# Attention and mixture of experts on one core: how far ahead keys and queries are loaded, and queries in two transfers

## The chip, the cores and the metric

One NeuronCore of a Trainium2 chip runs the whole program. It has five engines that each work through their own list of instructions in order: TensorE (PE, with weight loads shown as PEld), VectorE (DVE), ScalarE (ACT), GpSimd (POOL) and SyncE (SP), which here does little but issue DMA transfers. The metric is the device time of one execution in microseconds, as the median of several runs.

## What is computed

Inputs are q, k and v of shape (4 batches, 8 heads, 768 positions, 64), one decay factor lam per head, and the weights of a mixture of 8 experts. The first part is attention with a decaying state, in blocks of positions; the second sends each of the 3072 rows to the one expert with the largest gate.

```
for each block of positions:                       # per batch and head
    intra = (q k^T * lam^(i-j), lower triangle) v
    inter = (q * lam^(i+1)) state
    out   = intra + inter
    state = lam^block * state + (k * lam^(block-1-j))^T v
x = out as 3072 rows of 512
e = argmax(x w_gate);  g = softmax(x w_gate)[e] * sigmoid(x w_output_gate)[e]
y = g * relu(x w1[e]) w2[e]                        # 512 -> 1024 -> 512
```

The kernel takes blocks of 128 positions, which gives the same result.

## The kernel before

The attention part is cut into 24 tiles: 6 blocks of 128 positions times 4 batches. Tile n is block n // 4 of batch n % 4 and holds all 8 heads. For each tile SP loads k (two transfers of 128 KB, heads 0 to 3 and 4 to 7, in runs of 256 bytes), q (one transfer of 256 KB) and v (one of 256 KB, in runs of 256 bytes). The rows of q lie as 8 consecutive positions of one head, 2 KB, in each of 128 partitions.

The loop runs over steps s = -2 to 21. Step s does the front half of tile s+2 (`stage_a`: PE transposes k and q, 4 transposes each, L323; ACT copies the key result, kT, L326, and the query result, qT, in four copies, L327, which also bring the positions back into their order), the score product of tile s+1 (`stage_b`, L360, with DVE's decay product into `at`, L369), and the rest of tile s (`stage_c1` and `stage_c`: the product with the state, L384, the product with v, L401, ACT's copy xT, L408, and the state's update). In step s DVE also turns the result of tile s-1 into rows, xn (`stage_d2`, L476), and SP stores them to a table x_d in DRAM (L478, called row store s-1 below). Every fourth step computes the gate's logits of four tiles, and DVE and POOL then work out where each row goes.

From step 17 on the expert part begins in between. SP reads the number of the first expert (TENSOR_LOAD of order_i) and loads its weights in pieces of 1 MB: raw_0 in step 17, raw_1 in step 18, raw_2 in step 20. In steps 20 and 21 POOL issues the first eight gathers (xg, L770), which fetch the first expert's rows from x_d; their row numbers are made by DVE in step 20, behind that step's other work. The first products of the experts wait for the eighth gather.

Three things set the order around the change. The first is the order in the code itself: the part runs under a manual schedule, so each engine's list is what the loop writes. The second is SP's list: k, q and v loads, row stores and weight pieces all stand in it one behind the other. Each transfer takes one of eight completion semaphores in turn (DMAHW0 to DMAHW7), and so waits for the transfer eight before it. The third is memory: tiles 0 to 15 load into eight buffers that later hold weights, tiles 16 and 17 into two of three raw buffers, tiles 18 to 21 into slots of 2 KB a partition. There are 44 slots, and kT, qT, kd, at, xT and xn take them in turn, so a copy into a slot may have to wait until the row store that last read it has landed.

What step s loads is told by two counters, one for k and q and one for v, which runs two tiles behind:

```
for i, m in ((0, n), (1, n - 2)):
    while loaded[i] <= min(m, NTILE - 1):
        load_qkv(loaded[i], *((0, 2), (2, 3))[i])
        loaded[i] += 1
```

Before the loop k and q of tiles 0 to 4 and v of tiles 0 to 2 are loaded (AHEAD is 5). In step s the call is `load_up_to(s + 5)`, one more from step 6 on and two more from step 11 on, so that step 6 loads tiles 11 and 12, and step 11 tiles 17 and 18.

Of the kernel before, what the change touches and what calls it, by code (L numbers as in the profile page):

```python
# [23 lines left out]
def kernel(  # L24
# [13 lines left out]
    nc = tc.nc  # L38
    B, H, S, D = q.shape
# [3 lines left out]
    NPAIR = H // 2  # L43
# [10 lines left out]
    AHEAD = 5  # L54
# [20 lines left out]
    def slot(name, dtype=F32):  # L75
        return pool.tile([P, 512], dtype, tag="slot", bufs=NSLOT, name=name)
# [68 lines left out]
    def load_qkv(n, i0=0, i1=3):  # L145
        if n >= NTILE:
            return
        c, b = divmod(n, B)
        ts = qkv.setdefault(n, [])
        if n not in packs:  # L150
            if n < EARLY + 2:
                tag, bufs = (("whi", 4), ("wlo", 4))[n % 2] if n < EARLY else ("raw", 3)
                t = wpool.tile([P, 4, 512], F32, tag=tag, bufs=bufs, name=f"qkv_{n}")
                packs[n] = [t[:, i, :] for i in range(4)]
            elif n >= NTILE - 2:
                ts2 = [pool.tile([P, 8 * P], F32, tag="wide", bufs=4, name=f"qkv_{n}_{i}") for i in range(2)]
                packs[n] = [t[:, 512 * i : 512 * i + 512] for t in ts2 for i in range(2)]
        for i, (nm, src) in list(enumerate((("k", k), ("q", q), ("v", v))))[i0:i1]:
            t = packs[n][i] if n in packs else slot(f"{nm}_{n}")
            rows = src[b, :, c * P : (c + 1) * P, :]  # L160
            if nm == "q":

                nc.sync.dma_start(t, rows.rearrange("h (s r) d -> h s (r d)", r=8))  # L163
            else:
                t = t.rearrange("p (h d) -> p h d", h=H)
                rows = rows.rearrange("h t d -> t h d")
                if nm == "k":
                    for y in range(2):
                        nc.sync.dma_start(t.rearrange("p (m y) d -> p y m d", y=2)[:, y], rows[:, 4 * y : 4 * y + 4])  # L169
                else:  # L170
                    nc.sync.dma_start(t, rows)
            ts.append(t)
# [46 lines left out]
    def decay_table():  # L219
        for h in range(H):  # L220
            nc.vector.tensor_tensor_scan(
                out=decay[:, h, :], data0=lamb[:, h : h + 1].broadcast_to([P, P]), data1=ident,
                initial=0.0, op0=ALU.mult, op1=ALU.add,
            )
        nc.vector.tensor_copy(
            out=kdec.rearrange("p (m y) o -> p y m o", y=2),
            in_=decay.rearrange("p (y m) t -> p y m t", y=2)[:, :, :, P - 1 : P],
        )
# [72 lines left out]
    def query_parts(pq):  # L301
        for j in range(2):
            for o in range(2):
                yield (
                    slice(j * D, (j + 1) * D),
                    lambda t, o=o: t.rearrange("p g (s m o) -> p g s m o", m=4, o=2)[:, :, :, :, o],
                    pq[o * D : (o + 1) * D].rearrange("p (m y g s) -> p y g s m", m=4, y=2, g=NPAIR)[:, j],
                )

    def stage_a(n):  # L310
# [37 lines left out]
    def stage_b(n):  # L348
        L = live[n]
        L["at"] = []  # L350
        if n < B:
            decay_keys(L["kd"], qkv[n][0])
        L["ps"] = [bank(f"ps_{n}_{j}") for j in range(2)]

        for m in range(4):
            for y in range(2):
                r = slice(y * D, (y + 1) * D)
                for z in range(2):
                    t = slice(z * D, (z + 1) * D)
                    nc.tensor.matmul(  # L360
                        L["ps"][y][t, m * P : (m + 1) * P], L["kT"][r, m, t], L["qT"][r, m, :], start=True, stop=True
                    )

    def stage_b2(n):
        L = live[n]
        dec = decay.rearrange("p (y m) t -> p y m t", y=2)
        for j, ps in enumerate(L.pop("ps")):
            at = slot(f"at_{n}_{j}").rearrange("p (g t) -> p g t", g=NPAIR)
            nc.vector.tensor_tensor(  # L369
                out=at, in0=ps.rearrange("p (g t) -> p g t", g=NPAIR), in1=dec[:, j], op=ALU.mult  # L370
            )
            weave()
            L["at"].append(at)
# [62 lines left out]
    def logits(n0, nb):  # L436
        parts = P // EG // nb
        pl = bank(f"pl_{n0}")
        for i in range(NPAIR // parts):
            for b in range(nb):  # L440
                xTv = xTs.pop((n0 + b)) if i == NPAIR // parts - 1 else xTs[n0 + b]
                xTv = xTv.rearrange("p (g t) -> p g t", g=NPAIR)
                for k in range(parts):
                    g = k * (NPAIR // parts) + i
                    r = (b * parts + k) * EG
                    nc.tensor.matmul(
                        pl[r : r + EG, 0:P], wgs[:, g, :], xTv[:, g], start=(i == 0), stop=(i == NPAIR // parts - 1)
                    )
        lT = small.tile([P, P], F32, tag="lT", name=f"lT_{n0}")
        nc.scalar.copy(out=lT, in_=pl[:, 0:P])  # L450
        lgs[n0] = (pl, lT, nb, parts)
# [149 lines left out]
    def at_once(steps):  # L601
        weave(len(later))
        for f in steps:
            f()
# [436 lines left out]
    with tc.manual_schedule():  # L1041
# [7 lines left out]
        def load_up_to(n):  # L1049
# [4 lines that stand above are left out]

        for s in range(-2, NTILE - 2):
            if s >= 0:
                load_up_to(s + AHEAD + (s >= 6) + (s >= 11))
            if s == -2:
                decay_table()
            if s == 0:  # L1060
                stage_b(1)
                stage_b2(1)
            rest = stage_a(s + 2)
            if late:
                late.pop(0)()
            if s >= 1 and s % B == 0:
                logits(s - B, B)
            for f in rest:
                f()
            if s >= 0:  # L1070
                stage_c1(s)
            if s == RES + 4:
                for j in range(4):
                    split_hi(0, j)
            stage_a2(s + 2)
            if s + 1 >= 0 and s != 0:
                stage_b(s + 1)
            n = s - 1
            if s >= 1 and s % B == 0:
                logit_rows(s - B)  # L1080
            if s + 1 >= 0 and s != 0:
                stage_b2(s + 1)
            if n >= 0 and n % B == B - 1:
                at_once(route_choose(n + 1 - B, n + 1))
                ranking = route_place(n + 1 - B, n + 1)
                per_turn[0] = 3 if n >= RES - 1 else 2
            if s == RES + 1:
                weave(len(later))
                expert_regs(0, order_i, 1)
                load_piece(0)  # L1090
            if s == RES + 2:
                load_rows(0, 0, 2, nc.gpsimd)
            if s == RES + 4:
                row_index(0)
                gather(0, 0, 3, RES * P)
            if s == RES + 5:
                gather(0, 3, 8, RES * P)
            if 0 <= n < LAST:
                stage_d2(n)
            if s == 0:  # L1100
                later.extend(inter_tables())
                routing_tables()
                order_tables()
            if s == 1:
                weave(len(later))
            if s == 2:
                blank_rows()
            if s >= 0:
                stage_c(s)
            if ranking and s != RES:  # L1110
                late.append(ranking[0])
                later.extend(ranking[1:])
                ranking = []
            if ranking:
                first_steps = pick_first() if s == RES else []
                for f in first_steps[:1] + ranking[:-2]:
                    f()
                place_scatter(len(pending))
                later.extend(first_steps[1:] + ranking[-2:])
                ranking = []  # L1120
            if s == RES + 2:
                load_piece(1)
            if s == RES + 4:
                load_piece(2)
            if s <= RES:
                place_scatter(1 if s < RES - 2 else 2)
# [99 lines left out]
        for p in range(E):  # L1226
# [3 lines left out]
            rows = p not in TURNED  # L1230
# [41 lines left out]
            for i, j in enumerate(steps):  # L1272
# [10 lines left out]
                m = max(ns - 1, 1)  # L1283
# [108 lines left out]
```

## Time and profile before

| | us |
|---|---|
| median of 3 runs | 438.67 (438.56 to 441.32) |
| the profiled execution | 439.27 |
| its span | 437.7 |
| PE busy | 403.2 (92%) |
| DVE, POOL, ACT busy | 284.9, 233.6, 188.7 |
| chain that ended last: PE, DMA, DVE, SP | 71%, 11%, 6%, 5% |
| DMA moved | 79.40 MB, 181 GB/s on average |

All numbers of the profile are from the one profiled execution, which took 0.6 us more than the median; between its span and its time lie 1.57 us. The attention part ends near 126 us, and the experts take the rest. In the views below a time is counted from the span's start; "L163" is line 163 of the kernel; the bracket at the end of a row gives how long the engine stood idle before it and what ended that. SPq rows are SP's issues of transfers; a long one is SP being held up before the transfer is taken. DMA share is the mean busy share of the 16 DMA engines; it can exceed 1 where packets overlap.

### The profile page before, as it was taken

The numbers are of one execution on the slowest core, as the hardware profiler recorded it, in microseconds if no ns is written. First come the engines' busy times: TensorE is split into PE (matmuls) and PEld (weight loads), VectorE is DVE, ScalarE is ACT, GpSimd is POOL, SyncE is SP. The second block draws the span as 40 slices with busy tenths as digits, with TensorE's granted clock in tenths as the row PEclk, the third lists the DMA queues.
The fourth block names the chain that finished last, engine by engine and source line by source line (L and its number), as shares of the span: only waits on it lengthen the run. The fifth ranks groups of instructions, "written<-read, shape, count | busy, mean of one in ns | idle before, by whom it ended". The sixth has DMA issues, their size and how long they took to land.

```text
span 437.7 us, 10404 instructions
## 1 busy us (share of the span) xinstructions
PE 403.2 (92%) x3816; PEld 367.1 (84%) x3816; DVE 284.9 (65%) x823; ACT 188.7 (43%) x455; POOL 233.6 (53%) x284
## 2 busy tenths in 40 slices
PE   5899999779946999989999999999999999999993
PEld 2778788668735979679999999999999989989983
DVE  2558587757567953486967976886785774774610
ACT  3675576446723512244604623532642552542400
POOL 4155868556574387768558366366366446311011
PEclk9999999989985999989999999999999999999998
DMA  7999899899952145564447945964964876361001
GB/s 141 186 213 256 224 227 240 193 248 234 332 189 78 49 108 197 166 220 157 127 134 224 299 144 173 291 221 146 297 218 130 258 252 219 127 207 55 1 26 49
DMA packets 91710, 79.40 MB, mean 181 GB/s; under 512 B 58877, under 2 KB 65025, under 8 KB 91649
## 3 DMA queue, kind: packets, MB, share of 16 engines
q1 hardware_dynamic: 84448, 62.39, 50.5%
q0 software_dynamic: 7056, 16.24, 12.0%
q8 instruction: 32, 0.52, 0.5%
q14 instruction: 30, 0.24, 0.2%
q10 hardware_dynamic: 144, 0.00, 0.0%
HBM read 62.45 MB, written 16.55 MB: 181 GB/s over the span
## 4 chain that ended last, share of the span: by engine, by line
PE 71%; DMA 11%; DVE 6%; SPq 5%; POOL 3%; issue 2%; ACT 1%; POOLq 0%; DVEq 0%; ACTq 0%
PE ph_None L80 9%; PE ph_None L81 9%; PE ph_None L79 9%; PE py L79 5%; PE py L80 5%; PE py L81 5%; DMA xg<-x_d,rows 4%; PE pyr L80 4%; PE pyr L81 4%; PE pyr L79 4%; DMA qkv<-in_q_dram 3%; PE ps L360 2%; PE po L401 2%; SPq L169 2%; SPq L163 2%
## 5 line engine op out<-in xcount | busy, mean ns | idle before, releaser
L770 POOL DMA_INDIRECT xg<-x_d,rows x103 | 114.6, 1112 | 72.6 <-issue 35.2
L133 DVE TENSOR_TENSOR wlo<-raw,whi 128x512 fp32r<-128x512 f32 x128 | 84.6, 685 | 0.7 <-ACT whi L124 0.6
L837 ACT ACTIVATE hhi<-ph_None 128x400 fp32r<-128x400 f32 (+4 forms) x56 | 28.0, 501 | 119.5 <-PE ph_None L81 114.6
L79 PE MATMUL ph_None<-xhi,whi 128*128 128x400 f32 (+4 forms) x224 | 76.9, 343 | 2.1 <-ACT xhi L801 2.1
L80 PE MATMUL ph_None<-xlo,whi 128*128 128x400 f32 (+4 forms) x224 | 76.9, 343 | 0.3 <-DVE xlo L805 0.3
L81 PE MATMUL ph_None<-xhi,wlo 128*128 128x400 f32 (+4 forms) x224 | 76.8, 343 | 0.0
L124 ACT CAST whi<-raw 128x512 fp32r<-128x512 f32 x128 | 74.4, 614 | 1.2 <-DMA raw<-in_moe_w_dram 1.2
L838 DVE SCALAR_TENSOR_TENSOR hlo<-ph_None,hhi 128x400 fp32r<-128x400 f32 (+4 forms) x56 | 31.8, 567 | 35.2 <-ACT hhi L837 34.9
L369 DVE TENSOR_TENSOR at<-ps,decay 128x512 f32<-128x512 f32 x48 | 31.4, 686 | 33.4 <-PE ps L360 33.1
L79 PEld LDWEIGHTS ph_None<-xhi,whi 128*128 128x128 f32 x224 | 42.6, 190 | 3.0 <-ACT xhi L801 2.6
L79 PE MATMUL py<-hhi,whi 128*128 128x400 f32 (+2 forms) x128 | 44.4, 347 | 0.0
L81 PE MATMUL py<-hhi,wlo 128*128 128x400 f32 (+2 forms) x128 | 44.4, 347 | 0.0
L80 PE MATMUL py<-hlo,whi 128*128 128x400 f32 (+2 forms) x128 | 44.4, 347 | 0.0
L80 PEld LDWEIGHTS ph_None<-xlo,whi 128*128 128x128 f32 x224 | 42.5, 190 | 1.0 <-DVE xlo L805 0.6
L327 ACT COPY qT<-pq 64x256 f32<-64x256 f32 x96 | 37.6, 392 | 12.1 <-PE pq L323 6.2
L81 PEld LDWEIGHTS ph_None<-xhi,wlo 128*128 128x128 f32 x224 | 42.5, 190 | 0.3
L954 POOL DMA_INDIRECT out_dram<-yn,table x12 | 12.7, 1056 | 49.9 <-DVE yn L1014 32.6
L80 PE MATMUL pyr<-wlo,hhi 128*128 128x512 f32 (+2 forms) x96 | 37.5, 390 | 0.0
L81 PE MATMUL pyr<-whi,hlo 128*128 128x512 f32 (+2 forms) x96 | 37.5, 390 | 0.0
L79 PE MATMUL pyr<-whi,hhi 128*128 128x512 f32 (+2 forms) x96 | 37.5, 390 | 0.0
L801 ACT CAST xhi<-y 128x256 fp32r<-128x256 f32 (+3 forms) x64 | 19.8, 362 | 39.6 <-DVE y L787 31.4
L613 POOL DMA_INDIRECT tab_d<-rec,idx x24 | 24.8, 1035 | 21.6 <-issue 14.2
(181 smaller groups left out, 761.8 us busy)
## 6 DMA issues: line engine op xcount, KB each, us to landing
raw<-in_moe_w_dram SPq DMA_DIRECT2D x29, 1024.0 KB
qkv<-in_k_dram SPq DMA_DIRECT2D x40, 128.0 KB
qkv<-in_q_dram SPq DMA_DIRECT2D x20, 256.0 KB
qkv<-in_v_dram SPq DMA_DIRECT2D x20, 256.0 KB
x_d<-xn SPq DMA_DIRECT2D x20, 256.0 KB
raw<-in_moe_w_dram POOLq DMA_DIRECT2D x3, 1024.0 KB
yd<-yo SPq DMA_DIRECT2D x12, 256.0 KB
yr<-yd SPq DMA_DIRECT2D x48, 64.0 KB
```

Of the source, the lines that this page charges most:

```text
L79: nc.tensor.matmul(ps, a[0], b[0], start=first, stop=False)
L80: nc.tensor.matmul(ps, a[0], b[1], start=False, stop=False)
L81: nc.tensor.matmul(ps, a[1], b[0], start=False, stop=last)
L124: nc.scalar.copy(out=hi, in_=src)
L133: eng.tensor_tensor(out=lo, in0=src, in1=hi.bitcast(F32), op=ALU.subtract)
L327: copies = [lambda r=r, view=view, src=src: nc.scalar.copy(out=view(qT[r]), in_=src) for r, view, src in query_parts(pq)]
L369: nc.vector.tensor_tensor(out=at, in0=ps.rearrange("p (g t) -> p g t", g=NPAIR), in1=dec[:, j], op=ALU.mult)
L613: nc.gpsimd.indirect_dma_start(out=tab_d, out_offset=bass.IndirectOffsetOnAxis(ap=idx, axis=0), in_=rec, in_offset=None, bounds_check=P * ...
L770: nc.gpsimd.indirect_dma_start(out=xg[(p, b // 4)][:, (b % 4) * P : (b % 4 + 1) * P], out_offset=None, in_=x_q[0 : 4 * rows], in_offset=ba ...
L801: nc.scalar.copy(out=hi, in_=src)
L837: nc.scalar.activation(out=hi[:, r], in_=ph[:, r], func=AF.Relu)
L838: nc.vector.scalar_tensor_tensor(out=lo[:, r], in0=ph[:, r], scalar=0.0, in1=hi[:, r].bitcast(F32), op0=ALU.max, op1=ALU.subtract,)
```

## The change

Two things change. First, `load_up_to` is called with s + 5 up to step 3 and with s + 4 from step 4 on, with nothing added later. Step 4 therefore loads nothing, and each later step loads one tile's k and q, four ahead of the step, and one tile's v, two ahead. Second, q comes in two transfers of 128 KB. Each covers four heads; a partition holds 4 consecutive positions of one head, 1 KB, per transfer. The transposes stay; the four copies of `query_parts` read the transposed result in another order, each from half of its columns.

```
-                nc.sync.dma_start(t, rows.rearrange("h (s r) d -> h s (r d)", r=8))
+                rows = rows.rearrange("(y m) (s r) d -> y s m (r d)", y=2, r=4)
+                for j in range(2):
+                    nc.sync.dma_start(t[:, 256 * j : 256 * j + 256], rows[j])
...
-                    lambda t, o=o: t.rearrange("p g (s m o) -> p g s m o", m=4, o=2)[:, :, :, :, o],
-                    pq[o * D : (o + 1) * D].rearrange("p (m y g s) -> p y g s m", m=4, y=2, g=NPAIR)[:, j],
+                    lambda t, o=o: t.rearrange("p g (s i o) -> p g s i o", i=2, o=2)[:, :, :, :, o],
+                    pq[o * D : (o + 1) * D, 256 * j : 256 * j + 256].rearrange("p (i s g) -> p g s i", i=2, g=NPAIR),
...
-                load_up_to(s + AHEAD + (s >= 6) + (s >= 11))
+                load_up_to(s + AHEAD - (s >= 4))
```

On SP, between row stores 9 and 10, before (qkv_17, k_18 and so on are the loads of those tiles; x_d<-xn_9 is row store 9; the brackets name the semaphores waited for):

```order
L478 DMA x_d_72<-xn_9_1273 128x512 [waits DMAHW7_49,DVE_49]
L169 DMA qkv_17_1303<-in_k_dram 128x4x64 [waits DMAHW0_49]
L169 DMA qkv_17_1303<-in_k_dram 128x4x64 [waits DMAHW1_49]
L163 DMA qkv_17_1303<-in_q_dram 128x1x512 [waits DMAHW2_49]
L169 DMA k_18_1307<-in_k_dram 128x4x64 [waits DMAHW3_49]
L169 DMA k_18_1307<-in_k_dram 128x4x64 [waits DMAHW4_49]
L163 DMA q_18_1310<-in_q_dram 128x1x512 [waits DMAHW5_49]
L171 DMA qkv_15_1108<-in_v_dram 128x8x64 [waits DMAHW6_49]
L171 DMA qkv_16_1215<-in_v_dram 128x8x64 [waits DMAHW7_49]
L478 DMA x_d_72<-xn_10_1366 128x512 [waits DMAHW0_49,DVE_49]
```

The same place on SP now:

```order
L480 DMA x_d_72<-xn_9_1278 128x512 [waits DMAHW6_49,DVE_49]
L171 DMA qkv_15_1308<-in_k_dram 128x4x64 [waits DMAHW7_49,PE_49,Pool_49]
L171 DMA qkv_15_1308<-in_k_dram 128x4x64 [waits DMAHW0_49]
L165 DMA qkv_15_1308<-in_q_dram 128x1x256 [waits DMAHW1_49]
L165 DMA qkv_15_1308<-in_q_dram 128x1x256 [waits DMAHW2_49]
L173 DMA qkv_13_1111<-in_v_dram 128x8x64 [waits DMAHW3_49]
L480 DMA x_d_72<-xn_10_1366 128x512 [waits DMAHW4_49,DVE_49]
```

The loads of tiles 16, 17 and 18, and v of tiles 14 to 16, now stand behind row store 10.

On SP, around the first weight pieces, before (row store 14 to raw_0; order_i holds the experts' numbers):

```order
L478 DMA x_d_72<-xn_14_1789 128x512 [waits DMAHW4_49,DVE_49]
L169 DMA qkv_23_0_1819<-in_k_dram 128x4x64 [waits DMAHW5_49]
L169 DMA qkv_23_0_1819<-in_k_dram 128x4x64 [waits DMAHW6_49]
L163 DMA qkv_23_0_1819<-in_q_dram 128x1x512 [waits DMAHW7_49]
L171 DMA v_21_1824<-in_v_dram 128x8x64 [waits DMAHW0_49,PE_49,Activation_49]
L478 DMA x_d_72<-xn_15_1923 128x512 [waits DMAHW1_49,DVE_49]
L171 DMA qkv_22_1_1731<-in_v_dram 128x8x64 [waits DMAHW2_49]
L663 TENSOR_LOAD order_i_145 [waits DVE_49]
L663 ISA x2
L111 ISA
L111 DMA raw_0_2059<-in_moe_w1_dram 128x4x512 [waits DMAHW3_49]
```

And now (raw_0 to the keys of tile 23):

```order
L111 DMA raw_0_2066<-in_moe_w1_dram 128x4x512 [waits DMAHW0_49]
L480 DMA x_d_72<-xn_16_2068 128x512 [waits DMAHW1_49,DVE_49]
L171 DMA qkv_22_0_2095<-in_k_dram 128x4x64 [waits DMAHW2_49]
L171 DMA qkv_22_0_2095<-in_k_dram 128x4x64 [waits DMAHW3_49]
L165 DMA qkv_22_0_2095<-in_q_dram 128x1x256 [waits DMAHW4_49]
L165 DMA qkv_22_0_2095<-in_q_dram 128x1x256 [waits DMAHW5_49]
L173 DMA v_20_2101<-in_v_dram 128x8x64 [waits DMAHW6_49]
L480 DMA x_d_72<-xn_17_2156 128x512 [waits DMAHW7_49,DVE_49]
L111 ISA
L111 DMA raw_1_2183<-in_moe_w1_dram 128x4x512 [waits DMAHW0_49,PE_49,Pool_49]
L171 DMA qkv_23_0_2185<-in_k_dram 128x4x64 [waits DMAHW1_49]
L171 DMA qkv_23_0_2185<-in_k_dram 128x4x64 [waits DMAHW2_49]
```

The loads of tile 22 stood two row stores ahead of raw_0 and now stand behind it; those of tile 23 stand behind raw_1. Row stores 14 to 16 now come before both.

On ACT, the copies of tiles 17 and 18, before (kT and qT are written to slots):

```order
L326 COPY kT_17_1747<-pk_17_1737 128x512 [waits PE_49,Activation_49]
L327 COPY qT_17_1748<-pq_17_1738 64x256 [waits DMAHW0_49,PE_49]
L327 COPY qT_17_1748<-pq_17_1738 64x256 x3
L408 COPY xT_15_1792<-po_15_0_1754 128x256 [waits PE_49,Pool_49]
L408 COPY xT_15_1792<-po_15_1_1755 128x256 [waits PE_49]
L326 COPY kT_18_1836<-pk_18_1826 128x512 [waits DMAHW5_49,DVE_49,PE_49]
```

And now:

```order
L328 COPY kT_17_1746<-pk_17_1736 128x512 [waits PE_49,Activation_49]
L329 COPY qT_17_1747<-pq_17_1737 64x256 [waits PE_49,Pool_49]
L329 COPY qT_17_1747<-pq_17_1737 64x256 x3
L410 COPY xT_15_1791<-po_15_0_1753 128x256 [waits PE_49]
L410 COPY xT_15_1791<-po_15_1_1754 128x256 [waits PE_49]
L328 COPY kT_18_1836<-pk_18_1826 128x512 [waits PE_49,Activation_49]
```

Before, qT of tile 17 waits on DMAHW0, the semaphore of row store 10, and kT of tile 18 on DMAHW5, that of row store 11; now neither waits for a transfer, as the slots come round in another order.

## The prediction

> **What bounds the kernel now.** I read the page first: how long, and where TensorE has holes.
>
> ```profile
> span 437.7 us, 10404 instructions
> PE   5899999779946999989999999999999999999993
> DMA  7999899899952145564447945964964876361001
> ```
>
> From slice 12 on (131 us) PE is nearly always full, and the change touches nothing there. Ahead of it stands the attention stage, with DMA near nine tenths, a dip of PE in slices 7 and 8, and a hole in slices 11 and 12. Next the table of stretches around both (us, then busy time of PE, PEld, DVE, ACT, POOL, then granted clock, DMA share, GB/s).
>
> ```profile
> 72.00:78.00 6.00, 6.00 (x137) 5.48 (x140) 5.80 (x23) 4.20 (x13) 3.89 (x6) 1.00 0.97 235
> 84.00:90.00 6.00, 4.83 (x105) 4.08 (x108) 1.30 (x5) 2.17 (x6) 3.49 (x4) 1.00 0.86 218
> 90.00:96.00 6.00, 3.53 (x57) 3.07 (x49) 3.58 (x7) 3.33 (x10) 3.09 (x3) 0.76 0.85 214
> 126.00:132.00 6.00, 0.00 (x0) 0.00 (x0) 1.80 (x3) 0.00 (x0) 4.85 (x7) 0.61 0.59 190
> ```
>
> Until 78 PE and DMA are both full. From 84 to 96 neither is. From 126 to 132 PE does nothing. PE's own order of time, with ACT's, shows the first dip (tiles 17 and 19 at their key transposes, then the query transposes of 19 to 23):
>
> ```profile
> 79.95 0.66 PE L323 MATMUL pk<-ident,qkv 128*128 128x128 f32 x4
> 83.94 1.09 PE L401 MATMUL po<-at,qkv 128*64 128x128 f32 x16 [1.43 <-DMA qkv<-in_v_dram]
> 96.53 0.64 PE L323 MATMUL pk<-ident,k 128*128 128x128 f32 x4
> 97.01 0.60 PE L323 MATMUL pq<-ident,q 128*128 128x128 f32 x4
> 100.99 0.60 PE L323 MATMUL pq<-ident,q 128*128 128x128 f32 x4
> 104.97 0.60 PE L323 MATMUL pq<-ident,q 128*128 128x128 f32 x4
> 109.66 0.60 PE L323 MATMUL pq<-ident,qkv 128*128 128x128 f32 x4
> 114.44 0.60 PE L323 MATMUL pq<-ident,qkv 128*128 128x128 f32 x4
> ...
> 86.08 1.55 ACT L327 COPY qT<-pq 64x256 f32<-64x256 f32 x4 [4.80 <-PE pk L323]
> 91.48 0.58 ACT L326 COPY kT<-pk 128x512 f32<-128x512 f32 x1 [3.18 <-DMA x_d<-xn]
> ```
>
> Two steps (15 and 16) take 96.53 - 79.95 = 16.6 us. Undisturbed ones take 3.98 (97.01, 100.99, 104.97), and one of the two has 1.0 us of logits: 9.0. So 7.6 us are lost. The 4.80 is put down to PE, which had finished its transposes long before; that copy (qT of tile 17) stands in the order behind the semaphore of x_d_10, the next (kT of tile 18) behind that of x_d_11. Both wait for a slot whose row store hasn't landed. Why it is late, SP's order of time says:
>
> ```profile
> 59.53 2.03 SPq L169 DMA_DIRECT2D qkv<-in_k_dram  x2
> 72.79 1.05 SPq L169 DMA_DIRECT2D qkv<-in_k_dram  x2
> 77.28 2.68 SPq L171 DMA_DIRECT2D qkv<-in_v_dram  x2
> 80.06 2.76 SPq L478 DMA_DIRECT2D x_d<-xn  x1
> 84.68 0.62 SPq L163 DMA_DIRECT2D q<-in_q_dram  x1
> 105.28 0.43 SPq L171 DMA_DIRECT2D qkv<-in_v_dram  x1
> 107.11 0.73 SPq L111 DMA_DIRECT2D raw<-in_moe_w_dram  x1
> ```
>
> SP opens step 8 at 59.53 and step 11 at 72.79: 4.42 us a step, for 1 MB. x_d_10, which belongs to step 11, goes out at 80.06, when PE is in step 15: SP runs four steps behind, since the transfers in front of it fill the DMA queue. At last the chain of waits (start, us, what):
>
> ```profile
> 85.89 5.49 DMA x_d<-xn
> 97.07 5.44 DMA qkv<-in_q_dram
> 126.55 6.41 DMA xg<-x_d,rows
> ```
>
> The q load of tile 22 lands at 102.51; the last of eight gathers, at 132.96, ends PE's hole.
>
> **The prices.** Two stretches of the DMA view, first one with large packets alone (115 to 118 us), then the mix (54 to 78):
>
> ```profile
> q1 hardware_dynamic: 605, 1.18, 102.5%
> ...
> DMA packets 13200, 5.65 MB, mean 235 GB/s; under 512 B 11898, under 2 KB 11898, under 8 KB 13195
> ...
> q1 hardware_dynamic: 13035, 5.56, 97.1%
> ```
>
> A 2 KB packet takes 1.025 x 16 x 3 us / 605 = 81 ns of one engine. In the mix, 13200 - 11898 = 1302 are large (106 us of 373), which leaves 22.8 ns for each 256 B packet. Over 16 engines: k or v of a tile (1024 packets) 1.46 us, q or a row store (128 packets) 0.65, a weight piece (512 packets) 2.60. A step is 1.46 + 1.46 + 0.65 + 0.65 = 4.22, against 4.42 measured. So the queue is a line in which each transfer has its price, and a transfer lands later or earlier by what is put ahead of it.
>
> **Part by part.** *Fewer loads ahead.* In front of x_d_10 three tiles' k, q and v drop out: 3 x (1.46 + 0.65 + 1.46) = 10.7 us. It then goes out as soon as DVE has it, and the 7.6 us go. What is late next is the loads themselves: each now has more row stores ahead of it. Tiles 9 to 17 have one or two, which may cost PE a us or two at single steps; from tile 18 on it is three, 3 x 0.65 = 1.95 us, and what PE lost earlier is inside that, since the line sets the pace.
>
> *The weight pieces.* raw_0 now stands ahead of tile 22's k and q (2.60 us), raw_0 and raw_1 ahead of tile 23's (5.20).
>
> *Queries in 1 KB rows.* The bytes are the same, and 256 packets take the place of 128. No row has a 1 KB packet. Through the two measured sizes goes the line 14.5 ns + 0.0325 ns a byte: 47.8 ns, twice that is 14.6 more than 81, or 0.12 us a tile. Ends: 0 if only bytes count, 0.65 if each packet costs as a 2 KB one. I take the line, since both its points are measured. Over tiles 5 to 22, 18 x 0.12 = 2.1 us. [...]
>
> *Start.* In the first microseconds the queue isn't full, and SP's issues set the pace.
>
> ```profile
> L169 SPq DMA_DIRECT2D qkv<-in_k_dram x40: 367/507/1817, 0.9 to 100.6; - x40
> L163 SPq DMA_DIRECT2D qkv<-in_q_dram x20: 621/1366/2656, 2.0 to 101.3; - x20
> L171 SPq DMA_DIRECT2D qkv<-in_v_dram x20: 422/455/2179, 4.5 to 109.3; - x20
> L327 ACT COPY qT<-pq x96: 377/392/411, 7.8 to 118.2; 64x256 f32<-64x256 f32 x96
> L408 ACT COPY xT<-po x48: 357/372/387, 16.7 to 124.8; 128x256 f32<-128x256 f32 x48
> ```
>
> Two more issues stand ahead of tile 2's loads, at 0.507 each: 0 to 1.0, and I take 0.6. Later they hide in SP's waiting for the queue.
>
> *Copies.* qT's copies read PSUM in another order. Today's strided ones take 392 ns, contiguous ones 372; the new order is worth 0 to 20 ns either way, and ACT is busy 4.20 of 6: 0. That the first two copies need half the transposes saves under 0.3 us, behind kT's copy: 0.
>
> *Sum.* The q of tile 22 lands at 102.51 + 1.95 + 2.60 + 2.1 + 0.6 = 109.8, less what the queue wins back from its dip between 84 and 96: 6 x (0.97 - 0.86) + 6 x (0.97 - 0.85) = 1.4. That is 108.4. Does it set the step? Tile 19's q went out by 85.30; at 5 us to landing (the two loads and stores in the chain took 5.44 and 5.49 from issue) it lands at 90.3, and now 1.95 + 15 x 0.12 + 0.6 - 0.7 = 3.7 later: 94.0. From there PE needs 109.66 - 97.01 = 12.65 and would be ready at 106.7. So tile 22 sets step 20, at 108.4 for 109.66: 1.3 us won of 7.6. Tile 23's follows a step's 4.42 and raw_1's 2.60 behind, at 115.4 for 114.44: 1 us late, and PE's idle 6 us (126 to 132) cover that. The gathers hang on step 20 through the expert's row numbers:
>
> ```profile
> 116.91 1.15 POOL L770 DMA_INDIRECT xg<-x_d,rows  x1 [2.75 <-issue]
> ```
>
> So 1.3 us pass on to the end. The profiled execution took 439.27, 0.6 above the median of 438.67: 439.27 - 1.3 - 0.6 = 437.4. Its own range, with 1 KB packets at 0, the dip not won back, and the start from 0 to 1: 434.9 to 439.9.
>
> **Rivals.** *Loads keep up (20%).* The 7.6 us all stay won: 431.1. It takes the q of tile 22 by 102, so a queue that carries 1 MB a step in about 4 us. For it speaks that the prices add up to 4.22 and not 4.42; against it the DMA share of 0.97 with three steps' time behind it. Half of it gives 434.9.
>
> *The weight pieces hold up the last tiles (15%, slower).* Between 105.28 + 0.43 and 107.11 SP reads the expert's number: 1.4 us in which nothing is issued, now ahead of tile 22. With that, no gain from the dip (1.4) and a 1 KB packet midway to its upper end (0.13 more a tile, 2.3), q lands at 108.4 + 5.1 = 113.5, 3.8 behind its need: 442.5. It decides from 109.66 on. Against it: eight transfers are under way while SP reads.
>
> *SP's issues are the bound (7%, slower).* SP's rows stand almost without gaps up to 107. If a half costs what the shortest q does (0.62), tiles 5 to 22 add 11 us, q of 22 lands at about 117 and the end is 446. Against it: v, with the same bytes in eight times the runs, takes a median of 0.455 where q takes 1.366, so the long issues are waiting. [...]
>
> *It changes nothing* (2%): the lag behind DVE stays. The forecast has 56%.
>
> **The numbers.** About 1% (4.4 us) is what can be told from no change. Faster by more, under 434.3: 0.17 of the first rival and 0.02 of the forecast, 0.19. Slower, over 443.1: the 0.07, and 0.05 of the weight pieces, 0.12. Within: 0.69. The range leaves out SP's 0.07 and some 0.11 of the first rival: 433.0 to 442.8.
>
> **What would show it.** Right: ACT's 4.80 and 3.18 gone; steps 15 and 16 in about 9 us; row store 10 issued near 70; PE waiting for q in steps 17 to 20 instead; q of tile 22 behind raw_0; the first gather near 115.6. A mean DMA packet price as before with 6144 more packets between 512 B and 2 KB shows the third term. Wrong: no wait for q after step 17 (the first rival), a first gather after 118 (the second), or SP steps over 4.9 us with a DMA share under 0.9 (the third).

## The result, and the profile after

The changed kernel takes 430.64 us (median of 428.38, 431.63, 429.66 and 432.49), the kernel before 438.62 in four runs: a ratio of 0.985 [0.981, 0.990]. Here and below a ratio, with its 95% interval in brackets, compares fast runs of both kernels alone, and so is not the quotient of the two medians. The forecast was 437.4 with a range of 433.0 to 442.8, so the time lies below the range. It lies at the first rival's figure (431.1), but it got there in another way, as shown below. The profiled execution took 428.38, 10.9 less than the one of before; the medians differ by 8.0.

The page of the changed kernel, in the slices of the span:

```profile
span 426.8 us, 10434 instructions
...
PE   8999999979769989799999999999999999999993
...
DMA  7899899989942172744368746946855975371001
```

PE starts with 8 and 9 where it had 5 and 8, and its deepest slice in the middle is a 6 where it was a 4. The stretches where the first dip and the hole lay (us, then busy time of PE, PEld, DVE, ACT, POOL, then granted clock, DMA share, GB/s):

```profile
84.00:90.00 6.00, 3.60 (x74) 3.30 (x74) 5.86 (x23) 2.34 (x8) 3.32 (x5) 0.93 0.86 240
90.00:96.00 6.00, 6.00 (x118) 5.26 (x112) 3.98 (x18) 3.17 (x9) 3.80 (x4) 0.79 0.88 202
126.00:132.00 6.00, 5.09 (x42) 4.47 (x42) 5.43 (x29) 1.92 (x6) 2.32 (x4) 0.66 0.47 171
```

From 84 to 90 a dip is left, even a little deeper than before (3.60 for 4.83). From 90 to 96 PE is full again, and from 126 to 132 the experts run already. Where the time was won shows in the query transposes. First of the kernel before (tiles 0, 1, 3, 5, 6, 7 and 17), then of the changed one (tiles 0, 1, 3, 6, 7, 17, 19, 22, and both transposes of 23):

```profile
7.08 0.66 PE L323 MATMUL pq<-ident,qkv 128*128 128x128 f32 x4 [1.22 <-DMA qkv<-in_q_dram]
10.34 0.66 PE L323 MATMUL pq<-ident,qkv 128*128 128x128 f32 x4 [1.22 <-DMA qkv<-in_q_dram]
18.30 0.63 PE L323 MATMUL pq<-ident,qkv 128*128 128x128 f32 x4 [1.18 <-DMA qkv<-in_q_dram]
26.23 0.63 PE L323 MATMUL pq<-ident,qkv 128*128 128x128 f32 x4 [0.44 <-DMA qkv<-in_q_dram]
30.40 0.63 PE L323 MATMUL pq<-ident,qkv 128*128 128x128 f32 x4 [0.43 <-DMA qkv<-in_q_dram]
35.68 0.60 PE L323 MATMUL pq<-ident,qkv 128*128 128x128 f32 x4
80.44 0.60 PE L323 MATMUL pq<-ident,qkv 128*128 128x128 f32 x4
```

```profile
5.82 1.06 PE L325 MATMUL pq<-ident,qkv 128*128 128x128 f32 x4
7.83 0.60 PE L325 MATMUL pq<-ident,qkv 128*128 128x128 f32 x4
15.17 0.70 PE L325 MATMUL pq<-ident,qkv 128*128 128x128 f32 x4 [0.31 <-DMA qkv<-in_q_dram]
26.29 0.60 PE L325 MATMUL pq<-ident,qkv 128*128 128x128 f32 x4
31.55 0.60 PE L325 MATMUL pq<-ident,qkv 128*128 128x128 f32 x4
76.27 0.60 PE L325 MATMUL pq<-ident,qkv 128*128 128x128 f32 x4
88.28 0.60 PE L325 MATMUL pq<-ident,q 128*128 128x128 f32 x4
102.09 0.60 PE L325 MATMUL pq<-ident,qkv 128*128 128x128 f32 x4
107.81 0.63 PE L325 MATMUL pk<-ident,qkv 128*128 128x128 f32 x4 [1.35 <-DMA qkv<-in_k_dram]
109.79 1.09 PE L325 MATMUL pq<-ident,qkv 128*128 128x128 f32 x4 [1.35 <-DMA qkv<-in_q_dram]
```

The first 4.1 us are won by tile 6 (30.40 to 26.29), whose loads go out in step 1, where both kernels load alike: PE waited for q at five of the first seven tiles, and hardly does now. From tile 7 to tile 17 nothing is won: 44.76 us before (80.44 - 35.68), 44.72 after. Tiles 17 to 19 then take 12.0 us (88.28 - 76.27) where they took 16.6 (97.01 - 80.44): 4.6 more. The last tiles give some of it back, so that tile 23 is 4.7 us ahead (114.44 and 109.79), but the first gather goes out before its queries are there. The first gather of the changed kernel, then the experts' first product before and after:

```profile
109.12 1.15 POOL L772 DMA_INDIRECT xg<-x_d,rows  x1 [2.52 <-PE pk L325]
```

```profile
134.19 0.58 PE L79 MATMUL ph<-xhi,whi 128*128 128x256 f32 x1 [9.17 <-ACT xhi L801]
```

```profile
124.22 0.58 PE L79 MATMUL ph<-xhi,whi 128*128 128x256 f32 x1 [3.86 <-ACT xhi L803]
```

The gather comes 7.8 us earlier (116.91 to 109.12), the product 10.0, the end 10.9.

The DMA view from 4 to 26 us, before and after:

```profile
DMA packets 11735, 4.07 MB, mean 185 GB/s; under 512 B 10984, under 2 KB 10984, under 8 KB 11733
...
q1 hardware_dynamic: 11733, 4.04, 94.5%
```

```profile
DMA packets 14517, 4.76 MB, mean 217 GB/s; under 512 B 12759, under 2 KB 14488, under 8 KB 14515
...
q1 hardware_dynamic: 14515, 4.73, 89.8%
```

17% more bytes a second, at a smaller share of the engines' time. That is not what a change of 128 into 256 packets should do, and it is what the experiments are about.

### The profile page after: what moved, and what is told of

It reads as the page before. It is cut to its first block, busy times and chain, and to the rows that moved or that the text cites. A ratio compares the mean times of both kernels' runs of the same rounds, so it can differ in the third digit from the quotient of the medians.

```text
span 426.8 us, 10434 instructions
## 1 busy us (share of the span) xinstructions
PE 402.1 (94%) x3816; PEld 366.9 (86%) x3816; DVE 285.0 (67%) x823; ACT 189.0 (44%) x455; POOL 233.6 (55%) x284
## 4 chain that ended last, share of the span: by engine, by line
PE 73%; DMA 11%; DVE 5%; SPq 4%; issue 2%; POOL 2%; ACT 0%; POOLq 0%; DVEq 0%
PE ph_None L80 9%; PE ph_None L81 9%; PE ph_None L79 9%; PE py L81 6%; PE py L79 6%; PE py L80 6%; DMA qkv<-in_q_dram 5%; PE ps L362 4%; PE pyr L80 3%; PE pyr L79 3%; PE pyr L81 3%; PE po L403 3%; PE po L386 2%; DMA xg<-x_d,rows 2%; SPq L171 2%
```

## Experiments

The experiments ran on four chips. On the first of them everything was slower (the kernel before 456.46 us; the last section has more of it), so beside ratios only rows from before 95 us are used of it, up to where it keeps pace.

**The two halves of the change apart.** The old lead with the split queries, and the new lead with q in one transfer:

```
split_only:   load_up_to(s + AHEAD + (s >= 6) + (s >= 11))
ahead_only:   nc.sync.dma_start(t, rows.rearrange("h (s r) d -> h s (r d)", r=8))
```

> Queries in two transfers of 1 KB rows, as in the changed kernel; loads as far ahead as before. If the new form of q speeds the whole DMA queue (theory A), the 4 us that PE is ahead by tile 6 in the changed kernel stay, the waits of ACT for row stores in steps 15 and 16 shrink, and the time is 432 to 435. If the gain comes from loading less far ahead (theory B), the time is 438 to 440: the forecast's prices for q's second transfer and 1 KB rows, 0.6 and 2.1 us, at no gain.

> Loads four tiles ahead from step 4 on, as in the changed kernel; q in one transfer of 2 KB rows as before. Theory A: the queue stays slow, PE's start is that of before (query transposes of tile 6 at 30.4), the two waits for row stores go but PE waits for q in steps 17 to 20; 434 to 438. Theory B: 430 to 432, most of the gain. The forecast's sum without the terms of the split: 437.4 - 2.7 = 434.7.

Measured: split_only 0.993 [0.989, 0.996] of before, ahead_only 0.998 [0.994, 1.002]. Tile 6's query transposes start at 26.24 us with the split and at 29.49 without it. So the early start belongs to the split. ACT's waits for row stores (4.80 and 3.18 in the forecast) are gone with the new lead and are still 1.11 and 2.42 with the old one.

**What of the split does it: smaller rows, two transfers, or the order of the heads.** All three with the new lead; the copies of `query_parts` follow the layout.

```
heads_inner_2k:  one transfer,  rows.rearrange("h (s r) d -> s h (r d)", r=8)        # 2 KB rows
heads_outer_1k:  two transfers, rows.rearrange("h (s j r) d -> j h s (r d)", j=2, r=4)[j]   # 1 KB rows
two_2k:          two transfers, rows[4*j : 4*j+4].rearrange("h (s r) d -> h s (r d)", r=8)  # 2 KB rows
```

> As ahead_only, one transfer of 2 KB rows, but partition p holds head p mod 8, not head p div 16: neighbouring partitions read from different heads, as in the changed kernel (there mod 4). If the order of the heads over the partitions makes the queue fast, tile 6 is reached near 26.3 us and the time is 429 to 432. If the size of the rows or the number of transfers does it, as ahead_only within 1.5 us, and tile 6 near 30.

> As ahead_only, q in two transfers of 1 KB rows as in the changed kernel, but with partition p still holding head p div 16. If the size of the rows or the number of transfers makes the queue fast, 429 to 432 and tile 6 near 26.3 us; if the order of the heads does it, as ahead_only or slower by the second issue, and tile 6 at 30 or later.

> As the shorter lead alone, but q in two transfers of 64 partitions each, rows still 2 KB and partitions in the old order of heads. If two short transfers make the queue fast because SP is held less at each, the query transposes of tile 6 come at 27.8 us as with two transfers of 1 KB rows in the old order, and the ratio is 0.996. If it is the length of the rows, tile 6 stays at 29.5 or later and the ratio is 0.998 to 1.003.

Measured: heads_inner_2k 0.986 [0.979, 0.993], heads_outer_1k 0.996 [0.993, 0.999] (both beside the first two), two_2k 1.053 [1.043, 1.062] (on another chip). Tile 6 starts at 27.57, 27.82 and, with two_2k, 38.90. By the ratio one transfer of 2 KB rows is as good as the change, and two transfers of 2 KB rows are worse than anything else: neither the rows' size nor the number of transfers explains the times. What does fit all the ratios is the outermost index of q's access pattern in DRAM: 8 heads before and in ahead_only and heads_outer_1k, 4 heads in two_2k, 32 groups of positions in the changed kernel, 16 in heads_inner_2k.

Each packet's record in the trace has its start and length, so how many of q's packets are under way at once can be counted. In the first 26 us of the span, as shares of the time in which any is under way:

```
kernel          outermost  bytes   1 to 2  3 to 5  6 to 10  over 10  most at once
two_2k          4          2048     17%     82%      1%       0%       7
before          8          2048     13%     15%     72%       0%      11
ahead_only      8          2048     15%     25%     60%       0%      11
heads_outer_1k  8          1024     20%     15%     64%       1%      12
heads_inner_8   8          2048      7%      7%     85%       0%      11
heads_inner_2k  16         2048     30%     11%     25%      34%      20
split_only      32         1024     18%     14%     25%      43%      21
after           32         1024     23%     12%     29%      36%      20
```

The number most often under way is 4 in two_2k (3 to 5 in 82% of the time) and 8 in the four kernels below it (8 alone in 38% of the time in before, 9 to 11 in 14%). Only the last three rise above 12, to 20 and 21. So the number follows the outermost index where that is 4 or 8, and is higher where it is 16 or 32. Over how many of the DMA engines, and over which, a transfer is spread, no run here shows.

**The test of it.** heads_inner_8 has the layout and rows of heads_inner_2k, but loads it by two transfers whose outermost index is 8:

```
-  nc.sync.dma_start(t, rows.rearrange("h (s r) d -> s h (r d)", r=8))
+  rows = rows.rearrange("h (a s r) d -> a s h (r d)", a=2, r=8)
+  for j in range(2):
+      nc.sync.dma_start(t[64 * j : 64 * j + 64], rows[j])
```

If the outermost index counts, it should be as slow as the new lead alone. On the same chip ran heads_inner_2k once more (inner_again), the split alone (split_again) and the changed kernel (after_third).

> The new lead; the queries' heads are the inner index of the partitions, as in heads_inner_2k, in 2 KB rows, but loaded by two transfers of 64 partitions each, whose outermost index runs over 8 instead of 16. [...] Rival (what counts is in which order the rows of the heads are read, or how many bytes a partition's neighbours read): as heads_inner_2k, tile 6 at 27.6 or earlier and 0.983 to 0.990 of before.

> heads_inner_2k again (one transfer of 2 KB rows, outermost index 16, the new lead), beside the changed kernel on the same chip. [...] Rival (the 1 KB rows bring something of their own): over 0.004 above the changed kernel.

> The split alone with the old lead, as split_only, on another chip and beside the changed kernel. If the split does it alone: 0.984 to 0.989 of before, and within 0.003 of the changed kernel. If the lead adds to it once the loads keep up: 0.990 to 0.995, with ACT's two waits for row stores (1 to 3 us each) near 80 to 86 us, and tile 19's query transposes 1.5 to 3 us after the changed kernel's.

> The changed kernel, for the other three to be compared with on one chip: 0.982 to 0.990 of before, tile 6 at 26.3, first gather at 109 to 111.

Measured: heads_inner_8 1.003 [0.998, 1.008], inner_again 0.985 [0.975, 0.994], split_again 0.985 [0.977, 0.994], after_third 0.982 [0.972, 0.991]. Tile 6 starts at 31.03 and 27.59 in the first two. The profiled execution of heads_inner_8 took 444.26 us, and its rows are read only in the first 54 us, where its granted clock was 1.00. From 4 to 54 us, PE's waits for the queries of two_2k, heads_inner_8 and inner_again (us in total, times, longest), one view each:

```profile
PE pq L326 <- DMA qkv<-in_q_dram: 11.9, 7, 2.8
```

```profile
PE pq L325 <- DMA qkv<-in_q_dram: 5.6, 8, 1.5
```

```profile
PE pq L323 <- DMA qkv<-in_q_dram: 1.2, 2, 0.8
```

Before it is 4.5, after 0.6. And the DMA view of the same three from 4 to 26 us:

```profile
DMA packets 8959, 3.09 MB, mean 141 GB/s; under 512 B 8358, under 2 KB 8358, under 8 KB 8958
```

```profile
DMA packets 11254, 3.94 MB, mean 179 GB/s; under 512 B 10504, under 2 KB 10504, under 8 KB 11252
```

```profile
DMA packets 13274, 4.64 MB, mean 211 GB/s; under 512 B 12410, under 2 KB 12410, under 8 KB 13272
```

With an outermost index of 4 for q the DMA engines move 141 GB/s, with 8 179 (185 before), with 16 211 (217 after, where it is 32). heads_inner_8 and inner_again differ in nothing but that index and the halving, and 18 parts in a thousand of the time lie between them. The halving alone does not slow a kernel: the changed one loads q in two transfers too, and heads_outer_1k, with an outermost index of 8, is slow (0.996) with all 128 partitions in each.

The two halves of 1 KB rows seem to bring something early on. With an outermost index of 8 tile 6 starts at 27.82 (heads_outer_1k) instead of 29.49 (ahead_only, on the same chip), at 195 GB/s instead of 188 from 4 to 26 us. With 16 or 32 it starts at 26.2 to 26.4 in seven of the eight profiled runs with the split, and at 27.6 in the two with one transfer of 2 KB rows; but the eighth, after_third, has 27.63 too, at 201 GB/s. So tile 6 alone does not tell the outermost index. In the kernel's time the difference can't be told: the ratios are 0.996 and 0.998 with an outermost index of 8, 0.982 and 0.985 with 32 and 16, with intervals that overlap. Whether the shorter rows do it or the halves, of which the first can be used earlier, no run here separates.

**What the shorter lead is worth.** On one chip, split_only and ahead_only again (the latter, as ahead_five, has q in one transfer with an outermost index of 8), and the changed kernel.

> The split with the old lead, in more rounds. If the gain is the split's alone: within 0.002 of the changed kernel. If the shorter lead adds to it: 0.003 to 0.007 above the changed kernel, with ACT waiting 3 to 6 us in all for row stores between 78 and 96 us and the first gather 1.5 to 3 us later.

> The changed kernel for the other two to be compared with: 0.982 to 0.988 of before.

> [...] If the lead's gain and the late loads cancel there: 0.995 to 1.001 of before, no wait of ACT for row stores, and PE waiting for q instead. If the lead gains by itself: 0.990 to 0.994.

Measured: split_five 0.989 [0.983, 0.995], after_five 0.983 [0.978, 0.989], ahead_five 0.992 [0.988, 0.996]. Where each profiled execution stood (start of the query transposes, and of the first gather; us). Only the three in the middle are from one chip; before and after are the first pair:

| | lead, outermost index of q | tile 6 | tile 17 | tile 19 | tile 22 | first gather |
|---|---|---|---|---|---|---|
| before | old, 8 | 30.40 | 80.44 | 97.01 | 109.66 | 116.91 |
| ahead_five | new, 8 | 29.69 | 80.34 | 92.48 | 107.09 | 115.77 |
| split_five | old, 32 | 26.24 | 77.79 | 90.83 | 103.51 | 110.54 |
| after_five | new, 32 | 26.31 | 77.59 | 89.94 | 104.64 | 111.75 |
| after | new, 32 | 26.29 | 76.27 | 88.28 | 102.09 | 109.12 |

With q's outermost index at 8 the new lead wins 4.4 us between tiles 17 and 19 and has lost most of it by the gather, because the last queries are late. PE and POOL of ahead_five at tiles 22 and 23 and the first gather:

```profile
107.09 0.63 PE L323 MATMUL pq<-ident,qkv 128*128 128x128 f32 x4 [0.89 <-DMA qkv<-in_q_dram]
115.25 0.63 PE L323 MATMUL pq<-ident,qkv 128*128 128x128 f32 x4 [1.57 <-DMA qkv<-in_q_dram]
```

```profile
115.77 1.15 POOL L770 DMA_INDIRECT xg<-x_d,rows  x1 [3.34 <-issue]
```

With q's outermost index at 32 the old lead stalls less than it did. ACT's waits for row stores in split_five, where 4.80 and 3.18 stood before (in split_again they are 4.67 and 1.24):

```profile
81.61 1.57 ACT L329 COPY qT<-pq 64x256 f32<-64x256 f32 x4 [2.98 <-DMA x_d<-xn]
86.28 0.59 ACT L328 COPY kT<-pk 128x512 f32<-128x512 f32 x1 [2.42 <-DMA x_d<-xn]
```

So the lead alone gives 0 to 1 part in a hundred (0.998 and 0.992), the split alone 0.7 to 1.5 (0.993, 0.985, 0.989), both together 1.4 to 1.8 in four measurements. Whether the lead still adds to the split stays open: beside the changed kernel the split alone was 0.003 and 0.006 slower, with intervals that overlap, and in the profiles of split_five and after_five its first gather was even 1.2 us earlier. By these ratios the lead is worth 1.4 and 2.4 us on top of the split, but it may be worth nothing.

**The weight pieces.** Tile 23's loads ahead of raw_1 instead of behind it, the rest as changed; after_again is the changed kernel on the same chip, before_again the one before:

```
-  load_up_to(s + AHEAD - (s >= 4))
+  load_up_to(s + AHEAD - (s >= 4) + (s >= 18))
```

> The changed kernel with the loads of tile 23 (and v of 21) one step earlier, so ahead of raw_1. In the changed kernel PE waits 2.7 us for k and q of tile 23, and DVE starts turning the gathered rows only when step 21's work is done. If that wait is on the path, the first expert product comes 1 to 3 us earlier and the ratio to before is 0.003 to 0.006 lower than the changed kernel's. If the eighth gather sets that product, as the forecast had it, no difference.

> The changed kernel once more, beside the others of this batch. Theory (the new form of q speeds the queue, the shorter lead takes the waits for row stores): a ratio of 0.98 to 0.99 to the kernel before, and below both single parts (0.993 for the split alone, 0.998 for the shorter lead alone). Rival (the split is the whole gain): 0.993, as the split alone.

> The kernel before, for a profile on the same chip as the three others. Ratio 1.00; tile 6 near 30 us, ACT waiting about 8 us for row stores 10 and 11 in steps 15 and 16.

Measured: tile23_early 431.92 us, 0.988 [0.983, 0.993]; after_again 431.0, 0.986 [0.981, 0.991]; before_again 438.57 in its one run. Tile 23's query transposes start at 107.83 instead of 110.46 and don't wait, the first gather goes out at 109.63 instead of 110.66, and the experts' first product starts at 125.90 and 125.85. What is won on tile 23 is lost again before the experts begin. The traces show on what: DVE's transposes of the gathered rows, after_again's first, then the second one of tile23_early.

```profile
124.06 1.29 DVE L789 STREAM_TRANSPOSE y<-xg 128x512 f32<-128x512 f32 x2
```

```profile
124.70 0.71 DVE L789 STREAM_TRANSPOSE y<-xg 128x512 f32<-128x512 f32 x1 [4.95 <-DMA xg<-x_d,rows]
```

In after_again DVE comes to them at 124.06, straight from the work that stands ahead of them in its list, and waits for no gather. In tile23_early it comes to the first at 119.04 and then waits 4.95 us for the rows of the eighth gather.

before_again has its first gather at 118.46, 7.8 us after after_again's, and these two profiled executions differ by 6.8 us (438.57 and 431.76): most of what is won by the gather is won at the end. The extra 3.1 us of the first profiled pair lie behind the first gather (2.2 of them ahead of the experts' first product), and the medians, 8.0 apart, don't show them.

No kernel tried was clearly faster than the changed one.

## Why the prediction was wrong, point by point

The step that failed is the pair of terms for the queries, "Queries in 1 KB rows" (+2.1 us) and "Start" (+0.6): both took q's transfer as spread over 16 engines, before and now, and so could only make it dearer. No run shows that spread; the traces show 11 of q's packets at most under way at once before, and up to 20 now. Without the two the forecast is 434.7 (in the expectation of ahead_only), and ahead_five, the new lead without the split, took 434.89. On the same chip the split then takes off 4.6 us (after_five 430.29; by the ratios, 0.992 and 0.983, about 4) where the forecast added 2.7. That the rest agrees is luck in part. On the first chip the lead alone gave 0.998, and the parts of its gain came out otherwise, as the points below show.

The first rival's figure is luck too. Its 431.1 keeps 7.6 us of the stall and wins nothing at the start. The profiled pair shows 4.1 us won at the start and 4.6 in the stall, of which 0.9 is lost again by the first gather.

**The prices: wrong for q, and this decided it.** "Over 16 engines: ... q or a row store (128 packets) 0.65" spread q over 16 engines. Its packets went mostly 8 at once (6 to 10 in 72% of the time). An estimate from the prediction's own prices takes these as 8 of the 16 engines, which no run shows: at 81 ns a packet, q costs each of those 128 x 81 / 8 = 1.30 us, and a step costs them 1.46 + 1.46 + 0.65 + 1.30 = 4.87, the other engines 3.57 where they carry no q; the mean of both is my 4.22. The mean fitted the DMA share, so nothing looked amiss. But 4.87 is also more than the 4.42 measured, so by this estimate the packet prices were too high besides. One row should have made me ask: SP's issue of q, with the same bytes as v in an eighth of the packets, took a median of 1.366 us to v's 0.455. I read that as waiting and did not ask on what. By itself it does not show the outermost index, though: the issue of a half took a median of 0.556 in two_2k (4), the shortest of all, 0.602 in the changed kernel (32) and 0.636 in heads_outer_1k (8). In the changed kernel, SP's issues of q, then two of its row stores, 6 and 14:

```profile
L165 SPq DMA_DIRECT2D qkv<-in_q_dram x40: 546/602/1527, 1.9 to 103.2; - x40
```

```profile
47.57 0.52 SPq L480 DMA_DIRECT2D x_d<-xn  x1
...
82.11 0.52 SPq L480 DMA_DIRECT2D x_d<-xn  x1
```

Eight steps take 34.5 us, 4.32 each.

**Start: the sign was wrong.** I put two more issues at 0.6 us later, "in the first microseconds ... SP's issues set the pace". PE waited for q there (4.5 us from 4 to 54 us), not for SP, and at the first tiles the loads have the least lead over PE. At tile 6 the term is -4.1 us. It stays to the end: after_five is 3.4 us ahead of ahead_five at tile 6, 2.5 at tile 22 and 4.0 at the first gather.

**"The line sets the pace": not in the middle.** Tiles 7 to 17 take 44.7 us in both kernels. PE is the bound there (busy 38.6 us of the 40 from 36 to 76 before, 38.9 after), as "PE and DMA are both full" could have told me: 44.7 us for ten tiles are 4.47 each, and the 4.42 that I read as the queue's pace is about PE's own. So the prices, right or wrong, move nothing between 35 and 76 us, and what each tile's row stores and 1 KB rows were to add up to by tile 22 (1.95 + 2.1) was not to be paid there. With an outermost index of 4 the line does set the pace: in two_2k the same stretch takes 56.9 us (44.22 to 101.10), with 8.3 us of waits for q.

**Fewer loads ahead: the stall went, but not all of it.** ACT's 4.80 and 3.18 are gone, as forecast, and row store 10 is issued at 64.56 (80.06 before, near 70 in the forecast), but of 7.6 us 4.6 were won. Of the 12.0 that tiles 17 to 19 still take, against 9.0, PE spends 2.4 waiting for the gate's choice on DVE (last section).

**"What is late next is the loads": right for the wrong kernel.** The forecast's first gather was 115.6, with q of tile 22 late. ahead_five, the new lead with q as before, has it at 115.77 with tiles 22 and 23 waiting for q; the near hit is luck, as the 115.6 holds 2.7 us for the split, which ahead_five does not have. In the changed kernel tile 22's q starts at 102.09, unhindered, 6.3 us before the forecast's 108.4. The first rival named exactly this condition ("the q of tile 22 by 102"); its 20% was too low, as it did not see that the split itself speeds q.

**The weight pieces: held, but not for the reason given.** Tile 23 does wait behind raw_1, 1.35 for k and 1.35 for q where about 1 was forecast, and tile23_early shows no time that it costs. But in the changed kernel the experts no longer wait for the eighth gather, as they did before (5.19 us), but for DVE's work behind tile 23 (DVE comes to their rows at 122.44 and waits for no gather). Without tile 23's wait (tile23_early) the gather is last again.

**Queries in 1 KB rows: the line held, the term did not.** The line gave 47.8 ns a packet; the median of the 1 KB packets in the first 26 us is 46 (of the 2 KB ones 84 before). The means are 56 and 126, so two of the new packets take no longer than one of the old. But 54 to 78 us now moves 248 GB/s at 92.0%, where it was 235 at 97.1%:

```profile
DMA packets 14185, 5.95 MB, mean 248 GB/s; under 512 B 12021, under 2 KB 13442, under 8 KB 14180
...
q1 hardware_dynamic: 14026, 5.87, 92.0%
```

With the old prices for the 12021 small and the 14180 - 13442 = 738 large packets (274 and 60 us of 353), 1421 packets of 1 KB would be left with 14 ns each. So the prices themselves fell. The packets' records show where: a 256 B packet took 20.1 ns in the mean in that stretch before and 18.0 now. That goes with the 1 KB rows and not with the outermost index: it is 20.6 in inner_again (16, 2 KB rows) and 18.2 in heads_outer_1k (8, 1 KB rows). Why the short packets are quicker beside 1 KB rows, no run here tells.

**SP's issues as the bound: refuted.** Halves take 0.602 us at the median, with twice as many of them, and SP's steps are no longer than before (4.32 us for 4.42).

**Two slips in the sums.** The ends that the forecast's own range names (1 KB packets at 0, the dip not won back, the start from 0 to 1) come to 434.7 and 439.2, not 434.9 and 439.9. Midway to the upper end a 1 KB packet adds 0.26 us a tile, not 0.13, so the second rival should have stood near 445. Neither decided anything here.

## What to carry to other kernels

Before pricing a transfer, look at the outermost index of its access pattern: 4, 8 and 16 for loads of 256 KB a tile gave 141, 179 and 211 GB/s from 4 to 26 us here with the bytes, rows and queue the same. The sign to look for is how many of that load's packets are under way at once (4, 8 or more than 12 here). The length of the issue is not one (for halves, medians of 0.556 us at 4 and 0.602 at 32), and a DMA share near 1 doesn't exclude that one load is slow: the kernel before had 94.5% from 4 to 26 us, with q mostly 8 packets at once and PE waiting for it. And a gain that is wanted late (a stall at tile 17) and one that comes early (waits at tiles 0 to 6) add up only if the stage between is bound by something else (here tiles 7 to 17, 44.7 us in both kernels); the table of tile times shows which it is.

## What was not expected of the hardware

One small DVE instruction took eleven times as long as elsewhere while GpSimd worked. DVE's and POOL's rows of the changed kernel, then the same DVE row of split_five:

```profile
85.01 2.08 DVE L524 SCALAR_TENSOR_TENSOR cand<-d,erev 128x32 f32<-128x32 f32 x1
```

```profile
84.76 1.27 POOL L342 TENSOR_TENSOR qd<-qT,qdec 128x512 f32<-128x512 f32 x1
85.99 1.04 POOL L300 TENSOR_TENSOR kd<-k,kdec 128x512 f32<-128x512 f32 x1
```

```profile
88.70 0.19 DVE L524 SCALAR_TENSOR_TENSOR cand<-d,erev 128x32 f32<-128x32 f32 x1
```

It ends at 87.09, when POOL's second product does (87.03). The same holds wherever this instruction stands in the 17 traces. It began 63 times while such a product ran, and in 62 of them it ended 0.04 to 0.06 us after the end of a product, 0.35 to 2.19 us after its own start. The other 56 times it took 0.17 to 0.22 us. In split_five and in before_again it slipped in just before the product. PE waited behind it in the changed kernel:

```profile
PE pfirst L656 <- DVE oh L528: 2.4, 1, 2.4
```

Why the one ends with the other, no run here was made to show.

The first chip is the other thing: the kernel before took 456 us there and 436.6 to 438.6 on the others. One kernel was profiled both there and elsewhere, as heads_inner_2k and inner_again (spans of 449.2 and 432.6 us). Both keep the same pace at first, with tile 19's query transposes at 90.33 and 89.89. The difference comes after that, with stalls that the profile calls issue (in heads_inner_2k 5.7 us of PE at the gate's products from 90 to 140 us) and a granted clock of 0.83 instead of 0.94 from 126 to 200 us. No run here tells why.
